# Splitting the activations of the first MoE into three tiles, one raw q buffer less, and a newly drawn order table

## The chip, the core and the metric

The kernel runs on one core of one Trainium2 chip. The metric is device time in microseconds (us) of one launch. The five engines that matter are TensorE (PE, with its weight loads as PEld), VectorE (DVE), ScalarE (ACT), GpSimd (POOL) and SyncE (SP), which only issues DMAs here; ACT issues some DMAs too.

## What is computed

Attention over 2 batches x 8 heads x 768 tokens x 64 with a hash mask (two tokens see each other only if the signs of six projections agree), then two feed-forward layers over the 1536 x 512 result:

```python
q_bucket = np.sum((np.einsum('bhsd,dk->bhsk', q, proj) > 0) * powers, axis=-1)   # k_bucket alike
scores = np.where(mask, scale * np.matmul(q, k.transpose(0, 1, 3, 2)), -1000000000.0)
attn = softmax(scores); x = attn @ v                              # 1536 x 512 after the heads are joined
h = np.maximum(np.maximum(x @ w1, x @ w2), x @ w3); x1 = h @ w_out  # first MoE, 512 -> 768 -> 512
h = x1 @ w_in; g = np.where(h > 0.0, h, np.exp(np.minimum(h, 0.0)) - 1.0); out = g @ w_out2   # 512 -> 2048 -> 512
```

All matmuls are made of pairs of f16 tiles (a rounded value and its remainder), so nearly each f32 result is followed by a cast to f16 and a subtraction that gives the remainder.

## The kernel before, in words

The work is cut into 6 chunks of 256 tokens. A chunk has 4 pairs of heads with 4 attention tiles each, so there are 96 attention tiles. One tile runs through: four score matmuls on PE into `s` (L596), the row maximum on DVE (L599) with two small scalings (L600, L602), the exponential on ACT into `P` (L604), the cast `hl` on ACT or DVE (L610, L612), the remainder `hl` on POOL or DVE (L615), a transposing DMA from SP into `PT` (L617), and 18 matmuls with v into `o` (L626 to L628). After two pairs the normalized result (`xn`, L648 and L649) is transposed into `xT`.

Ahead of that, `plan_qk` loads q (four heads, both pairs of two) and k (two heads), scales them, casts them into `natq` and `natk` with their remainders (L382, L384), transposes them on PE and makes the bits of the hash. `plan_v` does v, `plan_w13` and `plan_wo` split the weights of the first MoE, which DMAs load as `raww`.

`plan_moe1` takes one chunk: 18 up-projections of two blocks (in all 108 pieces of 12 matmuls, `mo<-xT,w`), three of which are joined by maxima on DVE into `hx` (L684; the first of three is a plain copy on ACT or DVE, L686 and L688), a cast (L693) and a remainder (L695) into `hT`, and 4 down-projections of 18 matmuls (`mo<-hT,wot`). `hT` is one tile for the whole chunk in a ring of one buffer: the next chunk's first cast has to wait for the last down-projection of the chunk before. The second MoE (`plan_moe2`, L759 on) follows when attention is closed.

The order of all this is written out. Every step is an operation with the engines that may run it; the string `ORDER` unpacks to a list of (operation, engine) pairs, and `emit` issues the program in that order, so each engine works in the order of the table and waits where a tile isn't there yet. SP and ACT issue DMAs in the same way: a DMA that waits holds up what the table puts behind it on its queue. Tiles come from rings with a number of buffers (`ring`, `Graph.buf`); in the kernel before, a ring's buffers go round in turn.

Of the kernel before, what the change touches and what calls it, by code (L numbers as in the profile page):

```python
# [12 lines left out]
F16 = mybir.dt.float16  # L13
# [4 lines left out]
ALU = mybir.AluOpType  # L18
# [12 lines left out]
class Graph:  # L31
# [5 lines left out]
    def buf(self, pool, shape, dt, tag, bufs, ordered=False):  # L37

        self.bufs_of[tag] = bufs
        b = Buf(tag, lambda: pool().tile(shape, dt, tag=tag, name=tag, bufs=bufs))  # L40
        return b

    def fixed(self, tile_, tag):

        self.bufs_of[tag] = 1
        return Buf(tag, lambda: tile_)
# [30 lines left out]
    def emit(self):  # L77

        raw = zlib.decompress(base64.b85decode(ORDER))
        n = len(raw) // 2  # L80
        assert n == len(self.ops)
        done = [False] * n
        for lo, hi in zip(raw[:n], raw[n:]):
            w = hi << 8 | lo
            o, e = self.ops[w >> 3], ENGINES[w & 7]
            assert e in o["eng"] and not done[o["i"]] and all(done[d] for d in o["deps"])
            done[o["i"]] = True
            for b in o["allocs"]:
                b.ap = b.make()
            o["fn"](e)  # L90
# [4 lines left out]
    "c-mD~O;{TD))(-DK~x6682n=Ji$P<=PX?m`Y9go+2r3w(fF^~s3-R`S9`R-&_AbQseI7Agi0vYnEW~CZHVd&?NScM%F2r^r_AbQRMKE26=|XH4?-}h~yl4LZbAIP{e&-Cs3?F48iBzG|KACkb8a;oU"  # L95
    "nZ1c5gwEpnUT*LLI~M=vGqWK)CqRV1M%}JoC8R=iWZv0}?(^+O%eTB%x7KF#to=DP<9|1MgvT!ezeim(J6g3^+pzK?SSUY^$<!B*;|ZE!CgfBzQB0^cv#q$;OPg|jr{_zSy)vcT=Vz;oqF?zN+iwVM"
    "^{ZjYae!3RrT>I;8e)QNDPLiZ&x@rAH<wf>)XQ}5?}RG;r1vdyH0f|2MpfOq?5{qxyt{no)9Q5bUmN0y!uyF`*<|<-JBYaGr%QA#jpdm!(rU@W+3C$U$di!??sJ#o<;mt}J1U*?^pDW6!4<~OL+)jB"
    "z`8PSmyLK&cGeuO5c<Zu5st{0yaH<=m<Xy0PWbcgai7*$w(0qo^}9W1jOE3@{_NHE>#5nWE9AB)5B86u2D8n!zARc;{aF-=N-WY3v313{=i|vgUb*K~W}ati(bfHA(=qAAFKvV;NwTG#db0V$+ik>q"
    "%J3b<WkEFN_+oSBP}#%A-bQ0qYkW4eYPUO_FE0ZEJ)xJ7x*zFF7Yi<T6saX?a|+eA=ZuN|tb7+&-xF?L2ErVJZXGj96cORlUR52sYfjj9Ld@VdcB3$7e+s3sX7+j5i0VbyLQF@7%?<O9BPYhXaocBN"
    "*__>JM|TUP3YXjT#acMxcL&aU4^PWhf*+y^RdhDSU)2sL3uvxOvD>ps?ly!tqRFr;5}h#*yD<E_S8gt*n?5BhwqFkC{*5epPLq&N<ICQUTk)tj7N0-&o!2S<S`#jQ?iYXmx-Q^3Nm@h^35s3H62aIr"  # L100
    "dPlO?w;~`|Yh<rqLefIhn+IFzR=Z=(zvTRDClpY==I?|Sj$@Z-TpeMek2Rv49d|hKPG^*?u9H8WslSqW?j?Og|5-Ts`qF4tFn@EXUtqR5hqG#nWu9_nqe0imK5xa(OA>@a;iZ+ZRLgR%y*VNZBljoj"
    "csQ{#dxD=le`#{L-yi>}^m}p?Q!!Pyc6c=qJWJHdNCyqUHN=#_Jp9kP-7p8kKmA-;rHh!l2}jhZy0D&FefIh9-F5R}t!4jwd3xh7&!66<h%p*_HoMxnE;~0l$T=PjQTkBV(yDE`!}a=`TG@_m&7a&G"
# [42 lines left out]
def vcopy(n): return n / 1.92 + 68  # L145
# [4 lines left out]
def act(n, ap=0, acc=0): return n / 1.2 + 93 + 93 * ap + 93 * acc  # L150
# [10 lines left out]
def lsh_attention_moe_kernel(ctx: ExitStack, tc: tile.TileContext, q, k, v, proj,  # L161
# [758 lines left out]
```

## Time and profile before

| | |
|---|---|
| median of 3 runs | 672.31 us (671.91 to 677.66) |
| the profiled execution | 675.43 us, its span 673.6 us |
| PE busy | 620.3 us, 92% of the span |
| DVE, ACT, POOL busy | 557.9, 439.1, 231.8 us |
| mean granted clock of TensorE | 0.976 |

The span runs from the first to the last instruction; the rest of an execution's time lies around it. Shares of busy time are means over stages that differ, so the stages are read one by one. A busy PE is not PE at its peak, since matmuls overlap and their ends are modelled.

### The profile page before, as it was taken

The page shows a single profiled execution, that of the slowest core. Times are in us where ns is not written, and L with a number is a line of the kernel's source. Part 1 is how long each engine was busy: PE and PEld are TensorE (multiplying, and loading weights), DVE is VectorE, ACT ScalarE, POOL GpSimd, SP SyncE. Part 2 cuts the span into 40 slices and gives each one's busy share as a digit, 9 for nine tenths or more (in the row PEclk, how much of TensorE's full clock was granted, in tenths as well). Part 3 has the DMA queues.
Part 4 walks back from the last instruction along what each step waited for, and adds up shares of the span by engine and source line. Part 5 has one row for each costly group of instructions (what it writes and reads, how often), then busy time and mean ns, then how long its engine had stood idle before and what let it go on. Part 6 is the DMA issues. An engine that isn't in the chain of part 4 may idle for free.

```text
span 673.6 us, 16529 instructions
## 1 busy us (share of the span) xinstructions
PE 620.3 (92%) x6414; PEld 479.0 (71%) x6414; DVE 557.9 (83%) x1541; ACT 439.1 (65%) x806; POOL 231.8 (34%) x198
## 2 busy tenths in 40 slices
PE   5777566989999999999999899999999999999997
PEld 4555454867888888788789788766676666676674
DVE  6898998979998887898884888888899897777584
ACT  4978786788887667767552667676677564343341
POOL 1263544566445656757651112021011111110110
PEclk9998777999999999999999999999999999999999
DMA  8899999977998777978985553432221000000102
GB/s 277 238 220 257 208 244 227 194 167 153 184 181 154 141 138 157 182 135 165 147 165 164 176 154 103 126 94 64 64 63 64 1 1 1 1 1 11 54 33 93
DMA packets 201119, 87.66 MB, mean 130 GB/s; under 512 B 167760, under 2 KB 195408, under 8 KB 201040
## 3 DMA queue, kind: packets, MB, share of 16 engines
q1 hardware_dynamic: 187860, 70.97, 49.5%
q10 hardware_dynamic: 13180, 15.63, 7.9%
q8 instruction: 50, 0.82, 0.6%
q14 instruction: 29, 0.24, 0.1%
HBM read 38.80 MB, written 3.15 MB: 62 GB/s over the span
## 4 chain that ended last, share of the span: by engine, by line
PE 73%; DVE 10%; DMA 8%; ACT 4%; issue 3%; POOL 1%; ACTq 0%; DVEq 0%; SPq 0%; POOLq 0%
PE mo L663 40%; PE out L799 18%; PE s L596 6%; DMA PT<-hl 6%; PE o L626 2%; PE o L627 2%; PE o L628 2%; DVE m L599 2%; DMA qb<-btq 2%; ACT P L604 1%; POOL hl L615 1%; PE mo L394 1%; DVE dc2w L520 1%; DMA rawk<-in_k_dram 1%; ACT junk L317 1%
## 5 line engine op out<-in xcount | busy, mean ns | idle before, releaser
L615 POOL TENSOR_TENSOR hl<-P,hl 128x768 f16<-128x768 f32 x84 | 140.9, 1682 | 125.2 <-ACT hl L610 65.3
L663 PE MATMUL mo<-xT,w 128*128 128x256 f16 x1296 | 152.3, 272 | 0.0
L663 PE MATMUL mo<-x1T,win 128*128 128x256 f16 x1152 | 136.1, 273 | 0.0
L663 PEld LDWEIGHTS <-w 128*128 128x128 f16 x1296 | 123.7, 98 | 16.5
L799 PE MATMUL out<-wo2t,gt 128*128 128x512 f16 x576 | 134.6, 379 | 0.0
L663 PEld LDWEIGHTS <-win 128*128 128x128 f16 x1152 | 112.0, 98 | 24.3
L604 ACT ACTIVATE P<-s,bias,scale 128x768 f32<-128x768 f32 x96 | 94.1, 987 | 31.9 <-DVE bias L602 24.8
L792 POOL TENSOR_TENSOR gt<-g,gt 128x256 f16<-128x256 f32 x50 | 34.9, 700 | 221.4 <-ACT gt L790 101.7
L599 DVE TENSOR_REDUCE m<-s 128x1 f32<-128x768 f32 x96 | 91.0, 951 | 16.4 <-PE s L596 14.8
L783 ACT ACTIVATE r<-mo,nih 128x256 f32<-128x256 f32 x96 | 45.1, 470 | 79.6 <-PE mo L663 73.1
L799 PEld LDWEIGHTS <-gt 128*128 128x128 f16 x576 | 55.2, 98 | 53.6
L596 PE MATMUL s<-ka,qa 128*128 128x384 f16 x192 | 52.6, 360 | 19.4 <-ACT P L604 19.2
L610 ACT CAST hl<-P 128x768 f16<-128x768 f32 x64 | 52.4, 829 | 27.5 <-DMA PT<-hl 21.7
L626 PE MATMUL o<-vt,PT 128*128 128x65 f16 x576 | 65.6, 200 | 2.9 <-DMA PT<-hl 2.3
L627 PE MATMUL o<-vt,PT 128*128 128x64 f16 x576 | 65.4, 200 | 0.0
L628 PE MATMUL o<-vt,PT 128*128 128x65 f16 x576 | 65.2, 199 | 0.0
L626 PEld LDWEIGHTS <-PT 128*128 128x128 f16 x576 | 56.2, 101 | 7.5 <-DMA PT<-hl 4.5
L786 DVE TENSOR_SCALAR uu<-e,sg 128x256 f32<-128x256 f32 x96 | 35.5, 369 | 28.9 <-ACT e L785 27.9
L627 PEld LDWEIGHTS <-PT 128*128 128x128 f16 x576 | 56.3, 102 | 2.4 <-issue 0.5
L628 PEld LDWEIGHTS <-PT 128*128 128x128 f16 x576 | 56.2, 103 | 0.0
L596 PE MATMUL s<-kb,qb 76*128 76x384 f16 x192 | 53.2, 362 | 1.3 <-DMA qb<-btq 1.3
L663 PE MATMUL mo<-hT,wot 128*128 128x256 f16 x432 | 50.2, 272 | 0.0
(195 smaller groups left out, 1080.0 us busy)
## 6 DMA issues: line engine op xcount, KB each, us to landing
raw<-in_moe_w_out_dram SPq DMA_DIRECT2D x11, 512.0 KB
raw<-in_moe_w_in_dram SPq DMA_DIRECT2D x10, 512.0 KB
raww<-in_moe_w_dram SPq DMA_DIRECT2D x9, 512.0 KB
raww<-in_moe_w_dram ACTq DMA_DIRECT2D x9, 512.0 KB
raw<-in_moe_w_in_dram ACTq DMA_DIRECT2D x6, 512.0 KB
out_dram<-ot SPq DMA_DIRECT2D x12, 256.0 KB
rawk<-in_k_dram SPq DMA_DIRECT2D x7, 384.0 KB
rawv<-in_v_dram SPq DMA_DIRECT2D x7, 384.0 KB
```

Of the source, the lines that this page charges most:

```text
L596: PE.matmul(ps.ap[:, h, :NK], lh[0:n, h0 + i, j], rh[0:n, i, h * CH:(h + 1) * CH], start=first, stop=not first)
L599: op({"V": vred(S)}, lambda e: V.tensor_reduce(out=m.ap, in_=ps.ap[:, :, :NK], op=ALU.max, axis=AX.XY), rd=[ps], wr=[m], prio=t + 80.5)
L604: op({"A": act(S, ap=2) - 42}, lambda e: A.activation(out=P.ap.rearrange("p (c n) -> p c n", c=2), in_=ps.ap[:, :, :NK], func=AF.Exp, scal ...
L610: A.copy(hl.ap[:, 0], P.ap)
L615: op({"G": gtt(S), "V": (vtt(S), -109.46)}, lambda e: eng[e].tensor_tensor(out=hl.ap[:, 1], in0=P.ap, in1=hl.ap[:, 0], op=ALU.subtract), r ...
L626: PE.matmul(oo, pt.ap[:, kt], vt.ap[:, i, kt, :D + 1], start=(kt == 0), stop=False)
L627: PE.matmul(oo[:, :D], pt.ap[:, kt], vt.ap[:, i, kt, D + 2:], start=False, stop=False)
L628: PE.matmul(oo, pt.ap[:, NS + kt], vt.ap[:, i, kt, :D + 1], start=False, stop=(kt == NS - 1))
L663: PE.matmul(o, lh(kk, x), rh(kk, y), start=(kk == 0 and pi == 0), stop=(kk == n - 1 and pi == 2))
L783: op({"A": act(NQ, ap=1) - 42}, lambda e, m=m, o=o, r=r: A.activation(out=r.ap, in_=o.ap[:, :NQ], func=AF.Relu, scale=nih.ap[:, m:m + 1]), ...
L786: op({"V": vts(NQ)}, lambda e, m=m, ex=ex, uu=uu: V.tensor_scalar(out=uu.ap, in0=ex.ap, scalar1=-1.0, scalar2=sg.ap[:, m:m + 1], op0=ALU.a ...
L799: PE.matmul(outs[j].ap, gt.ap[:, x, j * 128:(j + 1) * 128], wo2t[f].ap[:, y], start=(len(seen) == 1 and pi == 0), stop=(len(seen) == n and ...
```

## The change

Four things change. The activations `hT` of a chunk become three tiles of two blocks each: the first from a ring `hTa`, the other two from a ring `hTb`, each with two buffers. The ring of raw q has one buffer where it had two; the raw buffers of k and v stay at two. A ring is now a set of separate tiles, and the buffer that an operation gets is the free slot, or the one whose last use stands earliest in the table. The table itself is new: all operations are the same, but their order, and for many the engine, differs.

```diff
-        b = Buf(tag, lambda: pool().tile(shape, dt, tag=tag, name=tag, bufs=bufs))
+        b = Buf(tag, lambda slot: pool().tile(shape, dt, tag=f"{tag}{slot}", name=f"{tag}{slot}", bufs=1))
...
+                slots, last = held[b.ring], max(place[i] for i in b.users)
+                if len(slots) < self.bufs_of[b.ring]:
+                    slot = len(slots)
+                    slots.append(last)
+                else:
+                    slot = min(range(len(slots)), key=slots.__getitem__)
+                    assert slots[slot] < t
+                    slots[slot] = last
+                b.ap = b.make(slot)
...
-        raw = ring(at, [128, heads, n, D], "raw" + kind, 2, ordered=True)
+        raw = ring(at, [128, heads, n, D], "raw" + kind, 1 if kind == "q" else 2, ordered=True)
...
-        hT = ring(hp, [128, FM, 2, NQ], "hT", 1, F16)
+        hT = [ring(hp, [128, 2, 2, NQ], "hTb" if f else "hTa", 2, F16) for f in range(0, FM, 2)]
...
-               rd=[t], wr=[hT], two=True, prio=pr + -417.89)
+               rd=[t], wr=[hT[f // 2]], two=True, prio=pr + -417.89)
...
-                    rd=[hT] + [f"wo{f}" for f in range(FM)], wr=[o, t], prio=pr + h * 1.5 * dp + 7.99)
+                    rd=hT + [f"wo{f}" for f in range(FM)], wr=[o, t], prio=pr + h * 1.5 * dp + 7.99)
```

Counted over the whole program, the new table moves 11 of the 96 remainders `hl` and 9 of the 18 remainders `hT` from POOL to DVE, 7 casts `hl` from DVE to ACT, and smaller numbers of other steps either way. PE has the same 12,830 instruction rows, and the last 3,053 of them stand in the same order as before. Line numbers of the changed kernel are 10 higher than before from `emit` on (L615 is L625 there).

The first place is the start of SP's queue, which issues the first loads. Before:

```order
L372 DMA rawq<-in_q_dram 128x4x128
L372 DMA rawk<-in_k_dram 128x2x384 x2
L471 DMA rawv<-in_v_dram 128x2x384
L372 DMA rawq<-in_q_dram 128x4x128
L505 DMA raww<-in_moe_w_dram 128x4x256
L471 DMA rawv<-in_v_dram 128x2x384
L372 DMA rawk<-in_k_dram 128x2x384
L505 DMA raww<-in_moe_w_dram 128x4x256
```

The same place in the changed kernel:

```order
L382 DMA rawq_153<-in_q_dram 128x4x128
L382 DMA rawk_170<-in_k_dram 128x2x384
L481 DMA rawv_186<-in_v_dram 128x2x384
L382 DMA rawk_198<-in_k_dram 128x2x384
L382 DMA rawq_205<-in_q_dram 128x4x128
L481 DMA rawv_272<-in_v_dram 128x2x384
L515 DMA raww_275<-in_moe_w_dram 128x4x256
L515 DMA raww_293<-in_moe_w_dram 128x4x256
L382 DMA rawk_304<-in_k_dram 128x2x384
```

Behind the second `rawq` stand now two loads for v and the weights; with one buffer that load waits until the first q has been split into `natq`, and SP waits with it.

The second place is the first MoE's remainder, in the middle of the attention stretch. Before, on POOL, among the remainders `hl` of the attention tiles (numbers tell tiles apart):

```order
L615 TENSOR_TENSOR hl_4041<-P_3954,hl_4041 128x768
L615 TENSOR_TENSOR hl_4086<-P_3900,hl_4086 128x768
L695 TENSOR_TENSOR hT_3740<-hx_3836,hT_3740 128x2x256
L615 TENSOR_TENSOR hl_4132<-P_3985,hl_4132 128x768
L695 TENSOR_TENSOR hT_3740<-hx_4114,hT_3740 128x2x256
L384 TENSOR_TENSOR natk_4031<-rawk_3459,natk_4031 128x12x64
L615 TENSOR_TENSOR hl_4255<-P_4173,hl_4255 128x768
```

In the changed kernel, on DVE, among the row maxima and scalings of attention tiles (L609, L610, L612) and the sums for v:

```order
L705 TENSOR_TENSOR hTb0_4004<-hx2_3820,hTb0_4004 128x2x256
L312 TENSOR_SCALAR vs1_99<-mo0_4117 128x1
L612 TENSOR_SCALAR bias0_4121<-m2_4089,scale0_4091 128x1
L499 TENSOR_REDUCE vm1_101<-vs1_99 128x1
L314 TENSOR_SCALAR vs1_99<-vs1_99 128x1
L694 SCALAR_TENSOR_TENSOR hx0_4095<-mo1_4094,hx1_4023 128x512
L703 CAST hTb1_4175<-hx0_4095 128x2x256
L705 TENSOR_TENSOR hTb1_4175<-hx0_4095,hTb1_4175 128x2x256
```

The remainders `hTb` stand on DVE right behind their cast or their maximum (L694), where POOL made them before.

The third place is PE near the end of attention, where the fifth chunk's sum of squares (`hacc`, which sets the scale of its down-projection) is made with a matmul by `ones`. Before:

```order
L264 LDWEIGHTS ones
L264 MATMUL mo<-hacc,ones 128x1
L265 LDWEIGHTS ones
L265 MATMUL mo<-tinyc,ones 128x1
L663 LDWEIGHTS wot
L663 MATMUL mo<-hT,wot 128x256
```

The same place in the changed kernel:

```order
L274 LDWEIGHTS ones
L274 MATMUL mo_7352<-hacc_7128,ones 128x1
L275 LDWEIGHTS ones
L275 MATMUL mo_7352<-tinyc,ones 128x1
L673 LDWEIGHTS w_104
L673 MATMUL mo_7325<-xT_6903,w_104 128x256
```

Before, the down-projection (`hT,wot`) followed at once; now one piece of the next chunk's up-projection (`xT`, 12 matmuls) stands between, and one more stands ahead of the sum.

## Rows read from the trace of the kernel before

**Rows 1.** The page: the span in 40 slices, busy tenths; PEclk is the granted clock.

```profile
PE   5777566989999999999999899999999999999997
...
PEclk9998777999999999999999999999999999999999
```

**Rows 2.** Windows: us of each engine's busy time per stretch, instructions in brackets, clock, DMA share.

```profile
core 0: us, PE busy (x) PEld busy (x) DVE busy (x) ACT busy (x) POOL busy (x), PEclk, DMA share, GB/s
0.00:60.00 60.00, 40.24 (x484) 31.18 (x485) 49.56 (x146) 44.26 (x73) 20.87 (x27) 1.00 0.94 242
60.00:110.00 50.00, 33.80 (x389) 24.42 (x389) 46.79 (x122) 42.17 (x68) 25.76 (x17) 0.69 1.14 240
110.00:157.00 47.00, 38.55 (x517) 32.11 (x516) 39.49 (x105) 36.08 (x56) 25.23 (x17) 1.00 0.89 186
157.00:350.00 193.00, 190.78 (x2585) 163.10 (x2583) 166.56 (x416) 141.71 (x215) 115.12 (x79) 1.00 0.85 157
350.00:425.00 75.00, 72.13 (x720) 62.45 (x719) 58.05 (x165) 44.16 (x99) 11.58 (x11) 1.00 0.51 150
425.00:674.00 249.00, 244.77 (x1729) 165.71 (x1726) 197.48 (x592) 130.74 (x300) 33.22 (x48) 1.00 0.13 43
```

**Rows 3.** The chain that ended last, 95 to 165: start, us, what.

```profile
108.88 6.62 DMA PT<-hl
...
151.34 4.91 DMA PT<-hl
...
157.02 1.31 PE mo L663 x12
...
158.88 0.65 PE s L596 x4
```

**Rows 4.** Groups by line and form: count, busy us, mean ns of one, idle before.

```profile
L615 DVE TENSOR_TENSOR hl<-P,hl 128x768 f16<-128x768 f32 x12 | 13.2, 1099 | 0.4 <-ACT hl L610 0.3
...
L612 DVE CAST hl<-P 128x768 f16<-128x768 f32 x32 | 19.4, 608 | 1.6 <-ACT P L604 0.9 <-DMA PT<-hl 0.4 <-DMA qb<-btq 0.2
...
L695 DVE TENSOR_TENSOR hT<-hx,hT 128x512 f16<-128x512 f32 x3 | 2.6, 858 | 0.0
...
L688 DVE TENSOR_SCALAR hx<-mo 128x512 f32<-128x512 f32 x2 | 1.4, 692 | 1.9 <-PE mo L663 1.9
...
L615 POOL TENSOR_TENSOR hl<-P,hl 128x768 f16<-128x768 f32 x84 | 140.9, 1682 | 125.2 <-ACT hl L610 65.3 <-DVE hl L612 32.9 <-issue 11.3
```

**Rows 5.** Two lines alone: shortest, median and longest of their instructions, in ns.

```profile
L615 DVE TENSOR_TENSOR hl<-P,hl x12: 943/950/1932, 81.1 to 354.9; 128x768 f16<-128x768 f32 x12
...
L612 DVE CAST hl<-P x32: 545/554/1517, 34.6 to 354.3; 128x768 f16<-128x768 f32 x32
```

**Rows 6.** Timeline of PE, 368 to 386: start, us, instruction, idle before and its releaser.

```profile
375.27 0.16 PE L264 MATMUL mo<-w2acc,ones 128*128 128x1 bf16 x1 [0.78 <-ACT junk L317]
...
376.02 0.16 PE L264 MATMUL mo<-hacc,ones 128*128 128x1 bf16 x1 [0.52 <-ACT junk L317]
...
378.87 0.16 PE L264 MATMUL mo<-w2acc,ones 128*128 128x1 bf16 x1 [0.67 <-ACT junk L317]
...
383.73 0.18 PE L264 MATMUL mo<-w2acc,ones 128*128 128x1 bf16 x1 [0.72 <-DVE hx L717]
```

**Rows 7.** Timeline, 0 to 16: the first loads from SP, and the first q split.

```profile
3.12 0.47 SPq L372 DMA_DIRECT2D rawq<-in_q_dram  x1
...
7.31 0.69 DVE L384 TENSOR_TENSOR natq<-rawq,natq 128x512 f16<-128x512 f32 x1
...
11.05 0.37 SPq L372 DMA_DIRECT2D rawk<-in_k_dram  x1
```

**Rows 8.** Waits of the queue of SP, 0 to 157: us in total, times, longest.

```profile
SPq L617 <- POOL natq L384: 6.2, 3, 3.3
...
SPq L372 <- POOL natq L384: 1.8, 1, 1.8
```

**Rows 9.** Timeline of PE, 655 to 674: its last piece.

```profile
660.58 9.23 PE L799 MATMUL out<-wo2t,gt 128*128 128x512 f16 x42
```

More of the change, by code (lines that the diff above doesn't have):

```diff
@@ L45, in fixed @@
         self.bufs_of[tag] = 1
-        return Buf(tag, lambda: tile_)
+        return Buf(tag, lambda slot: tile_)
     def op(self, eng, fn, rd=(), wr=(), prio=0.0, two=False):
@@ L81, in emit @@
         assert n == len(self.ops)
-        done = [False] * n
-        for lo, hi in zip(raw[:n], raw[n:]):
-            w = hi << 8 | lo
+        place, held = {}, defaultdict(list)
+        todo = [(hi << 8 | lo) for lo, hi in zip(raw[:n], raw[n:])]
+        for t, w in enumerate(todo):
+            place[w >> 3] = t
+        for t, w in enumerate(todo):
             o, e = self.ops[w >> 3], ENGINES[w & 7]
-            assert e in o["eng"] and not done[o["i"]] and all(done[d] for d in o["deps"])
-            done[o["i"]] = True
+            assert e in o["eng"] and all(place[d] < t for d in o["deps"])
             for b in o["allocs"]:
-                b.ap = b.make()
+                slots, last = held[b.ring], max(place[i] for i in b.users)
[7 more added lines that the diff above has]
+                b.ap = b.make(slot)
             o["fn"](e)
@@ L99 @@
[L99 to L102, printed above, removed]
@@ new lines @@
+    "-aq8apG3}g{lQQsCyc}xEDVjrIdj6q?!lX537%A{zhpY}n0eAUukrrsTD83u24~jOzh4@{kw05}B>%iuwM?5qePVxb?-=_`QTeS|b0TuTOtr)sS2^h^IZa~Bkc#9c)n(B0dnmkPQ!CV@lN3ejSQrqX"
+    "zor*mU&u3L8QZ7aT#f2~o>m7Xq1Sq98J)MYKj+3pM{&L9i1TZuQiGY($)w)4_m=V6a^+1Q{<e}7zD>&v_#ZJg`|Q!=j(_%>Ov1w_?Z)CtD&vS0PNiSjKIHb3Po-j$@F%>^Fy{3+lneIh&A^^bZE$2<"
+    "nU737w{LDfX4{$Db<706#UinIG#;TY%_qFCgJfS~brn55dv9TTyoz5#U%pxkVuI7xYJKv+Y+v7d7nA($JX_rICX%TOpI`RmBmbc<DA=BI9jAYgvwqo_349ig{50*p%Eg4r&v$6*mwQ`!$$~s**^kUE"
+    "24~#9km^V^m)z<{Q1;R*iPp$VrLST;E0G^bMFzcN-hOToO7LII!ONv9m1$q>awnbPgoi}gSyD6YD|FoaR;jk@G1O_8T^ak>w!lx{VrPCbJDsj4(v7Hwbnumj#rIoW6qTCFKwrMuWw&^JiT#;aJis%U"
@@ new lines @@
+    "g^9RKxo!^}o#N`XBzJDXX-|D5to!!0)Eb`mR{A1(i{I@*Nzr|&VB0HCz4yKO``>YI!cJa8M874^lyvrm<3ra4wmKU;5K5=f^~_Nsx$(*JUwPrkVNUWz$`9AG$WEsJ;=v_fctqRsUX*<i6n?iCAcwZr"
+    "CAh@F-X--6NW!YC81e%@b~Q^qIps%oV+N+~ttN%$q*Ih1f3YAt=x&DWTJ}@V9}4i`dXC%dS(+NlNN}Z1<8;}k!){NR=GG6C6?FTHgRfq)_TI!-4BnMQG?qh+KS~^a%Cc6@9m`lVO7*1P!~2hA9u2PV"
+    "3qt`+*dO)=!rpIAPU8`dJ&`<nr<10lug-n`j2j_gAO5)(7xG-6EMOaME8Xj`Uo3uixyi<a4$BWx!-3D^kuUz`R|Rjm5=rrF9tlC^D~VLk0KPiE@xprHWO@JFEM1$$RiO^?%C1_zPVwu)2mQU_tF<>A"
+    "rwem${FhK7-;BhgN4X2kW3%mhZ>|1Bm9w^=jQkW$r8B3eDgn(&roNL<@H3^WF&^H3zAZ%0qh(*mGzRfiW$3+X+O56veCn0uC||5BBP@EH9XI!5$3}hNn_1CI^UiN#9DAiyU!9s)4e#vz9<R?73J09K"
@@ L142 @@
+    "(S+GYW41?QkH)U;adu7GpFw&$_SiuXj~{2*$AE2cj6*#>{`fi(_V~JZJo(s`h2u6b`%{~p$hL9FcKf*fp9Lk@<fMJlZoftVCZ9}BK6&!Q{?8&p)+Zr8efH#u<H=KCK?3S0lTRm~K79%q5ctzc2f;w+"
+    "*>(NI0qv*Ho?gdigk8rhA{vk#5F8(T@IiKgIUU#LbU2;Qi0T;>A3THN83>+bmCg_T8Tbb|ub~s1*yH~Ilz|{_"
 )
@@ L692, in plan_moe1 @@
                 prev = t
-            op({"V": vcopy(N2), "A": (act(N2), -91.99)}, lambda e, f=f, t=t: (V.tensor_copy if e == "V" else A.copy)(hT.ap[:, f:f + 2, 0], two_(t)),
-               rd=[t], wr=[hT], two=True, prio=pr + -417.89)
+            op({"V": vcopy(N2), "A": (act(N2), -91.99)}, lambda e, f=f, t=t: (V.tensor_copy if e == "V" else A.copy)(hT[f // 2].ap[:, :, 0], two_(t)),
+               rd=[t], wr=[hT[f // 2]], two=True, prio=pr + -417.89)
             op({"G": gtt(N2), "V": (vtt(N2), 391.34)}, lambda e, f=f, t=t: eng[e].tensor_tensor(
-                out=hT.ap[:, f:f + 2, 1], in0=two_(t), in1=hT.ap[:, f:f + 2, 0], op=ALU.subtract), rd=[t, hT], wr=[hT], two=True, prio=pr + 159.76)
+                out=hT[f // 2].ap[:, :, 1], in0=two_(t), in1=hT[f // 2].ap[:, :, 0], op=ALU.subtract), rd=[t, hT[f // 2]], wr=[hT[f // 2]], two=True, prio=pr + 159.76)
             square(t, lambda t=t: t.ap, N2, bufcol(hacc, f // 2), pr)
```

82 lines of the change are left out of this document (38 added, 44 removed).

## The prediction

> **What bounds the kernel now.** I read the page's slices first, then windows by stage, then the chain of waits. The slices of PE show three stages: a front in which PE is busy for five to eight tenths, a long stretch at nine, and an end at nine and a short tail [rows 1]. The windows give the amounts [rows 2]. Up to 157 us PE is idle for 60 - 40.24 = 19.8, 50 - 33.80 = 16.2 and 47 - 38.55 = 8.5 us, 44.4 in all, and from 60 to 110 its clock was granted at 0.69 on average, so for a good part at the lower of its two levels, 1.2 GHz. From 157 to 350 PE is idle for 2.2 us only, from 350 to 425 for 2.9, from 425 to the end for next to nothing but the 4 us after its last matmuls, which end near 669.8 [rows 9]. Matmul work is the same before and after, so the time can change only through the start of the saturated stretch, through the 5.1 us of gaps in it, or through new gaps. In the front DVE is the busiest engine: 49.56 of 60, 46.79 of 50, 39.49 of 47 us [rows 2]. It is idle for 10.4, 3.2 and 7.5 us there. From 60 to 110 it is the bound; from 110 to 157 the chain of waits passes through the transposing DMAs of the attention tiles, 4.91 and 6.62 us a piece in the rows shown, with the last one just before the first up-projection at 157.02 [rows 3].
>
> **What the change moves, and the sum.** I counted the new table's instructions on each engine up to the same attention tile and gave each the mean of its line and form [rows 4].
>
> *Front, DVE.* Up to the 25th row maximum DVE has 3.6 us more work than before, with two remainders `hl` moved over from POOL (2 x 1.099 = 2.2 us) as the largest item; the rest is scalings and splits of weights and raw tiles, and casts that went the other way. ACT has 4.4 us less, POOL the same. The place of the first up-projection in PE's order is one tile later, behind 26 score and 20 value pieces instead of 25 and 19. Where DVE is the bound (60 to 110, 3.2 us of idle time) the 3.6 us must be paid; in the 7.5 us of idle time behind 110 they can be hidden, by work that waits for transposes there. Bounds: +5.3 (all of it and more; the sum up to the 26th maximum is 5.3) and -7.5 (a table that fits the transposes better closes all that idle time). I take half of 3.6, +1.8.
>
> *One tile earlier.* The tile that now lies ahead of the first up-projection is work that the saturated stretch no longer has: its scores took 0.65 us, and its 18 matmuls with v fill the 0.55 us between the end of the up-projection piece at 158.33 and the scores at 158.88 [rows 3]. -1.2.
>
> *Middle, DVE.* From the 25th to the 96th row maximum DVE gets 9.9 us more: nine remainders `hl` (9.9), eight `hT` (6.9) and five first copies `hx` (3.5) come over, six casts `hl` (3.6) and a number of raw scalings, splits and casts (near 6.8 net) leave. POOL loses 24.7 us over the whole program, but it isn't waited for much: it is busy for 115.12 of 193 us [rows 2]. DVE is idle for 26.4 of those 193 us; the cover shrinks to 16.5. If PE's waits grow as the cover shrinks, 2.2 us become 2.2 x 26.4 / 16.5 = 3.5. I take +1.3, with bounds 0 (all hidden; each remainder is ready 1.682 - 1.099 = 0.6 us sooner [rows 4]) and +9.9 (none hidden, where the moved steps stand in front of a row maximum that PE's next scores wait for through ACT).
>
> *Gaps near 375.* PE waits four times for sums of squares or for the tile ahead of them, 0.78 + 0.52 + 0.67 + 0.72 = 2.7 us [rows 6]. In the new order two pieces of the sixth chunk's up-projection stand around the fifth chunk's sum, before its down-projection; a piece is 1.31 us [rows 3]. This covers the first two waits, -1.3; the other two are for the weights of the second MoE, which I leave. Bounds 0 and -2.7.
>
> *The q buffer.* The second q load, issued at 3.12 us, now waits for the end of the first q's split at 7.31 + 0.69 = 8.0, and two loads wait behind it on SP. The old queue stood still too, till 11.05 [rows 7]; the first weights also come by ACT's queue. On DVE the work up to the fourth row maximum is 3.4 us less than before. I take 0, between +3 (the load late by 4.9, less what the old stop hid) and -3.4.
>
> *Split tiles and rings by rule.* These issue no instruction. In the table the down-projections of the first four chunks still stand ahead of all up-projections of the next; the second buffers of `hTa` and `hTb` serve the late stretch above. The last 3,053 rows of PE, about from 440 us on, are unchanged: 0.
>
> Sum: +1.8 - 1.2 + 1.3 - 1.3 = +0.6. The profiled execution, 675.43 us, becomes 676.0; it lies 3.1 above the median of the runs, 672.31, so the forecast in terms of the median is **672.9 us**. A change under 1% (665.6 to 679.0) is about what a measurement of this kernel can't tell from none.
>
> **A rule against the trace.** The remainder on DVE took 950 ns in the median and up to 1932, the cast 554 and up to 1517 [rows 5]: some of them stand still for about a microsecond. The Trainium skill, page "SBUF — State Buffer", section "Who interferes with whom", says that a DVE instruction with two SBUF inputs and a GpSimd instruction that reads SBUF block each other for the whole of an instruction. The trace agrees as far as those longest cases go. By that rule every remainder moved to DVE meets those still on POOL, and at the worst length the eleven moved `hl` would cost 11 x (1.932 - 1.099) = 9.2 us more on DVE. By the mean of the row, which has such cases in it, nothing is added to the sum; and POOL's smaller share gives some of it back.
>
> **The rivals.**
>
> *DVE becomes the bound of the attention stretch (slower).* For it: 46.79 of 50 us before 110, and 86% rising to 91% from 157 to 350. Against it: 26.4 us of cover. It decides when the moved remainders stand ahead of row maxima at the wrong moment, so that half of their 9.9 us shows: 5.3 - 1.2 + 5.0 = +9.1 and no gain at 375, 681.4; with all of it 686. Chance 0.24, of which a fifth stays under 1%. The port rule above acts through this place too.
>
> *The front closes (faster).* For it: the chain runs through transposes and the casts and remainders around them, a remainder on DVE is ready sooner, ACT has 4.4 us less there, and the first row maxima come after less work. Against it: DVE has more. The first up-projection comes 7.5 us sooner: -7.5 - 1.2 - 2.7 + 1.3 = -10.1, 662.2. Chance 0.30, of which a sixth stays within 1%.
>
> *SP stands before a q load (slower).* With one buffer a load of q waits for the split of the group before. SP already stood for POOL's `natq` three times for 6.2 us, up to 3.3 at once, ahead of transposes [rows 8]. Two of the new q loads on SP lie among the front's transposes; 2 x 3.3 = +6.6 on top of the sum, 679.5. Against it: in most places the table has the split well ahead of the load. Chance 0.06.
>
> *The change does nothing that counts*: the buffers stay unused and the order evens out, 672.3; together with the forecast, 0.40.
>
> Within 1%: 0.40 + 0.05 + 0.05 + 0.02 = 0.52. Faster: 0.25. Slower: 0.23. The likeliest case's own range is 666 to 679; the range that should hold 8 of 10 reaches to the middle of the two main rivals' further parts, 661.5 to 684.
>
> **What would show it.** Windows of the changed kernel: the first `xT,w` piece between 155 and 160; PE idle between 2 and 5 us from there to 350; DVE busy for 9 to 11 us more in all, POOL for some 25 less; waits of PE near 375 down to about 1.4. The forecast is wrong if the first piece comes before 152 or after 163, if PE's waits in the middle pass 8 us, or if SP's waits for `natq` exceed 12 us in the front.

## The result, and the profile after

The changed kernel takes 678.75 us in the median of 20 runs (673.29 to 684.31), the kernel before 674.6 us in 20 runs beside it (671.91 to 678.08). The ratio is 1.0054, 95% interval 1.0034 to 1.0075: slower by about 3.6 us, and within the 1% that the forecast called no change. The ratio leaves out two of the changed kernel's runs, which lie more than 1.5% above its fastest, so it is a little nearer to 1 than the quotient of the medians. The profiled execution took 676.24 us, its span 674.4. Executions of one kernel lie up to 11 us apart, so the two profiles (span 673.6 before) show where time goes, and the ratios how much.

The page after, the slices that answer to [rows 1]:

```profile
PE   4766666999999999999999999999999999999997
...
PEclk9966687999999999999999999999999999999999
```

The first, third and fourth slices of PE are a tenth emptier, and the clock of the third and fourth was granted at 6 where 9 and 8 stood. Then the windows that answer to [rows 2], same columns:

```profile
core 0: us, PE busy (x) PEld busy (x) DVE busy (x) ACT busy (x) POOL busy (x), PEclk, DMA share, GB/s
0.00:60.00 60.00, 36.88 (x441) 28.12 (x441) 45.91 (x144) 38.94 (x62) 17.55 (x24) 0.88 0.91 237
60.00:110.00 50.00, 33.16 (x372) 23.46 (x373) 43.87 (x108) 41.01 (x64) 22.32 (x14) 0.67 1.00 213
110.00:157.00 47.00, 43.25 (x555) 35.22 (x553) 44.93 (x124) 40.75 (x60) 26.05 (x18) 0.96 0.98 210
157.00:350.00 193.00, 188.93 (x2523) 160.62 (x2521) 166.71 (x416) 146.24 (x226) 94.72 (x66) 1.00 0.85 158
350.00:425.00 75.00, 74.77 (x795) 65.23 (x794) 57.12 (x160) 46.53 (x99) 13.33 (x13) 1.00 0.59 155
425.00:674.00 249.00, 245.54 (x1737) 166.53 (x1734) 198.24 (x600) 135.40 (x309) 33.71 (x49) 1.00 0.13 43
```

From 0 to 60 us PE was busy for 3.4 us less and DVE for 3.7 us less; from 110 to 157 both were busy for about 5 us more. From 157 to 350 PE is idle for 193 - 188.93 = 4.1 us instead of 2.2, from 350 to 425 for 0.2 instead of 2.9.

The timeline of PE gives the first up-projection (start, us, instruction). Before:

```profile
112.51 1.47 PE L663 MATMUL mo<-xT,w 128*128 128x256 f16 x12
```

After:

```profile
121.81 2.78 PE L673 MATMUL mo<-xT,w 128*128 128x256 f16 x24
```

This is the place that the prediction read wrongly: its 157.02 us [rows 3] is the first piece that the chain of waits holds, not the first one on PE. The chain lists only its own pieces.

The loss arises earlier. DVE starts row maximum 7 at 47.3 us before and 47.9 after, 8 at 51.2 and 56.5, 10 at 57.0 and 66.0, 25 at 113.0 and 120.5. PE from 44 to 57 us after, with the idle time before an instruction and what ended it:

```profile
49.51 0.51 PE L404 MATMUL mo<-ident,natk 128*128 128x128 f16 x6 [0.37 <-POOL natk L394]
52.75 0.23 PE L636 MATMUL o<-vt,PT 128*128 128x65 f16 x1 [2.73 <-DMA PT<-hl]
...
53.73 0.20 PE L274 MATMUL mo<-gm,ones 128*128 128x1 bf16 x1
...
54.82 0.83 PE L404 MATMUL mo<-ident,natk 128*128 128x128 f16 x6
55.44 0.65 PE L606 MATMUL s<-ka,qa 128*128 128x384 f16 x2
```

And DVE over the same time:

```profile
49.55 0.68 DVE L530 SCALAR_TENSOR_TENSOR dc2w<-mo,dc2w 128x512 int32<-128x512 int32 x1
54.00 0.16 DVE L312 TENSOR_SCALAR swm<-mo 128x1 int32<-128x1 int32 x1 [3.77 <-PE mo L275]
...
56.45 0.96 DVE L609 TENSOR_REDUCE m<-s 128x1 f32<-128x768 f32 x1 [0.24 <-PE s L606]
...
63.44 0.95 DVE L609 TENSOR_REDUCE m<-s 128x1 f32<-128x768 f32 x1
```

A value piece (`o<-vt,PT`, the 18 matmuls of a tile with v) heads PE's queue and waits 2.73 us for its transposing DMA. Behind it stand a sum (L274) that DVE waits for, 3.77 us, six k transposes (L404) and the scores of tile 8 (L606), none of which need that `PT`. Counted from 44 to 110 us (wait: us in total, times, longest), the waits of value pieces for `PT` are new. After:

```profile
PE o L636 <- DMA PT<-hl: 10.7, 4, 3.4
...
DVE swm L312 <- PE mo L275: 6.6, 2, 3.8
PE s L606 <- ACT P L614: 5.4, 7, 2.1
```

Before, this wait isn't among PE's; the longest in total there is the scores' for the exponential, which after is down to 5.4 us:

```profile
PE s L596 <- ACT P L604: 10.1, 8, 3.9
```

Groups by line and form after, which answer to [rows 4]:

```profile
L625 DVE TENSOR_TENSOR hl<-P,hl 128x768 f16<-128x768 f32 x23 | 22.2, 968 | 0.7 <-ACT hl L620 0.3 <-issue 0.2
...
L622 DVE CAST hl<-P 128x768 f16<-128x768 f32 x25 | 13.9, 554 | 5.6 <-DMA PT<-hl 4.0 <-ACT P L614 1.3
...
L705 DVE TENSOR_TENSOR hTb<-hx,hTb 128x512 f16<-128x512 f32 x9 | 6.2, 694 | 0.4 <-ACT hTb L703 0.2
...
L698 DVE TENSOR_SCALAR hx<-mo 128x512 f32<-128x512 f32 x5 | 3.4, 675 | 0.0
...
L625 POOL TENSOR_TENSOR hl<-P,hl 128x768 f16<-128x768 f32 x73 | 123.4, 1697 | 143.0 <-ACT hl L620 82.7 <-DVE hl L622 33.7 <-issue 8.7
```

The counts moved as the prediction says, and POOL's busy time fell by 24.1 us to 207.7. But DVE's did not rise: 556.8 us after 557.9. The mean of a remainder fell from 1099 to 968 ns, that of a cast from 608 to 554. With the mean of each form as before, the counts of after would give about 10 us more. The typical instruction is no shorter, though; the two lines alone after (shortest, median, longest), against [rows 5]:

```profile
L625 DVE TENSOR_TENSOR hl<-P,hl x23: 946/951/1311, 70.0 to 357.0; 128x768 f16<-128x768 f32 x23
...
L622 DVE CAST hl<-P x25: 546/552/561, 31.4 to 355.5; 128x768 f16<-128x768 f32 x25
```

The medians are the same (950 and 554 before). What fell is the number of long ones: two remainders of 12 before (1741 and 1932 ns), one of 23 after (1311); three casts of 32 before (786 to 1517), none of 25 after. The longest remainder of before began while POOL worked:

```profile
349.46 1.16 POOL L721 TENSOR_TENSOR x1T<-hx,x1T 128x512 f16<-128x512 f32 x1 [1.33 <-ACT x1T L719]
349.50 1.93 DVE L615 TENSOR_TENSOR hl<-P,hl 128x768 f16<-128x768 f32 x1
```

PE near 375 us after, which answers to [rows 6]: of the four waits one is left.

```profile
378.37 0.17 PE L274 MATMUL mo<-w2acc,ones 128*128 128x1 bf16 x1
...
379.73 0.17 PE L274 MATMUL mo<-w2acc,ones 128*128 128x1 bf16 x1
...
380.13 0.16 PE L274 MATMUL mo<-hacc,ones 128*128 128x1 bf16 x1 [0.16 <-ACT junk L327]
...
383.45 0.17 PE L274 MATMUL mo<-w2acc,ones 128*128 128x1 bf16 x1
```

SP's waits from 0 to 157 us, which answer to [rows 8]:

```profile
SPq L382 <- DVE natq L394: 3.8, 1, 3.8
...
SPq L627 <- POOL natq L394: 2.6, 1, 2.6
```

The load of q now waits for its split for 3.8 us in one piece instead of 1.8, the transposes behind `natq` for 2.6 instead of 6.2; together 6.4 instead of 8.0.

### The profile page after: what moved, and what is told of

The parts are those of the page before. It is cut to its first block, busy times and chain, and to the rows that moved or that the text cites. A ratio compares the mean times of both kernels' runs of the same rounds, so it can differ in the third digit from the quotient of the medians.

```text
span 674.4 us, 16552 instructions
## 1 busy us (share of the span) xinstructions
PE 622.5 (92%) x6414; PEld 479.2 (71%) x6414; DVE 556.8 (83%) x1546; ACT 448.9 (67%) x816; POOL 207.7 (31%) x183
## 4 chain that ended last, share of the span: by engine, by line
PE 62%; DMA 15%; DVE 9%; ACT 7%; issue 3%; POOL 2%; ACTq 0%; SPq 0%; DVEq 0%; POOLq 0%
PE mo L673 34%; PE out L809 18%; DMA PT<-hl 12%; PE s L606 4%; ACT P L614 2%; POOL hl L625 2%; DVE m L609 2%; ACT hl L620 2%; DMA rawk<-in_k_dram 2%; PE o L636 1%; PE o L637 1%; PE o L638 1%; ACT junk L327 1%; PE mo L404 1%; DMA raw<-in_moe_w_in_dram 1%
## 5 line engine op out<-in xcount | busy, mean ns | idle before, releaser
L625 POOL TENSOR_TENSOR hl<-P,hl 128x768 f16<-128x768 f32 x73 | 123.4, 1697 | 143.0 <-ACT hl L620 82.7
L609 DVE TENSOR_REDUCE m<-s 128x1 f32<-128x768 f32 x96 | 91.0, 951 | 10.0 <-PE s L606 8.0
L636 PE MATMUL o<-vt,PT 128*128 128x65 f16 x576 | 66.9, 200 | 15.5 <-DMA PT<-hl 13.2
L636 PEld LDWEIGHTS <-PT 128*128 128x128 f16 x576 | 56.5, 102 | 20.3 <-DMA PT<-hl 15.1
L637 PE MATMUL o<-vt,PT 128*128 128x64 f16 x576 | 66.9, 201 | 0.0
L638 PE MATMUL o<-vt,PT 128*128 128x65 f16 x576 | 66.7, 200 | 0.0
L620 ACT CAST hl<-P 128x768 f16<-128x768 f32 x71 | 58.2, 827 | 7.9 <-DMA PT<-hl 6.9
L606 PE MATMUL s<-ka,qa 128*128 128x384 f16 x192 | 52.4, 358 | 11.6 <-ACT P L614 11.1
L606 PE MATMUL s<-kb,qb 76*128 76x384 f16 x192 | 52.7, 359 | 1.1 <-DMA kb<-btk 1.1
L798 DVE SCALAR_TENSOR_TENSOR g<-mo,aj,uu 128x256 f32<-128x256 f32 x96 | 46.1, 481 | 4.9 <-POOL gt L802 0.9
```

Source lines behind the costliest of these rows:

```text
L606: PE.matmul(ps.ap[:, h, :NK], lh[0:n, h0 + i, j], rh[0:n, i, h * CH:(h + 1) * CH], start=first, stop=not first)
L609: op({"V": vred(S)}, lambda e: V.tensor_reduce(out=m.ap, in_=ps.ap[:, :, :NK], op=ALU.max, axis=AX.XY), rd=[ps], wr=[m], prio=t + 80.5)
L620: A.copy(hl.ap[:, 0], P.ap)
L625: op({"G": gtt(S), "V": (vtt(S), -109.46)}, lambda e: eng[e].tensor_tensor(out=hl.ap[:, 1], in0=P.ap, in1=hl.ap[:, 0], op=ALU.subtract), r ...
L636: PE.matmul(oo, pt.ap[:, kt], vt.ap[:, i, kt, :D + 1], start=(kt == 0), stop=False)
L637: PE.matmul(oo[:, :D], pt.ap[:, kt], vt.ap[:, i, kt, D + 2:], start=False, stop=False)
```

## The experiments

All are built on the changed kernel's code; only the table and, where the old table needs it, the buffers differ. With the old table or a part of it, raw q has two buffers again and `hTa` one:

```diff
-        raw = ring(at, [128, heads, n, D], "raw" + kind, 1 if kind == "q" else 2, ordered=True)
+        raw = ring(at, [128, heads, n, D], "raw" + kind, 2, ordered=True)
-        hT = [ring(hp, [128, 2, 2, NQ], "hTb" if f else "hTa", 2, F16) for f in range(0, FM, 2)]
+        hT = [ring(hp, [128, 2, 2, NQ], "hTb" if f else "hTa", 2 if f else 1, F16) for f in range(0, FM, 2)]
```

Every ratio is to the kernel before on the same chip, with its 95% interval; two of these runs compared with each other mostly ran on different chips. A ratio isn't the quotient of two medians: they differ by up to 0.34%. Times of tiles are from one profiled execution each.

### Structure, buffers, and the two ends of the table

Four runs, with these tables:

```diff
-ORDER = new
+ORDER = old                                                  # old_table
+ORDER = new, and the edit above                              # new_q2
+ORDER = old[:622] + [x for x in new if x not in old[:622]]   # front_old: old to its 25th tile
+ORDER = new[:676] + [x for x in old if x not in new[:676]]   # front_new: new to its 28th tile
```

Old table on the new structure.

> The order table of the kernel before, on the new structure: hT split in three tiles (one buffer of hTa, two of hTb, the room of the old tile), rings as separate tiles given out by rule, two raw q buffers. Theory (the table makes the difference, first of all its front): as before, 0 to 1 us off 674.6. Rival (the split and the rule for buffers change waits by themselves): 2 us or more off.

Two raw q buffers under the new table.

> The new table with two raw q buffers; the room comes from the second hTa buffer, which is taken away. Rival theory (the single raw q buffer holds up SP and with it the front): the 25th row maximum comes 4 us or more sooner than in the changed kernel (120.5 us), and the time falls to 675 or less. Theory (order of the front, not the buffer): as the changed kernel, 677 to 680, the 25th row maximum within 2 us.

Old front, new rest.

> The old table up to its 25th attention tile, then all that is left in the order and on the engines of the new table. Theory (the new front costs, the new end gains 3 to 5 us near 375): 670 to 673. Rival (the 10 us more of DVE work between tile 25 and 96 cost): 676 to 679.

New front, old rest.

> The new table up to its 28th attention tile, then what is left in the order and on the engines of the old table. Theory (the new front costs, and here nothing gives it back near 375): 678 to 682, slower than the changed kernel or like it. Rival (DVE's work in the middle costs): 674 to 676, as before.

| run | median, us | ratio |
|---|---|---|
| old table throughout | 675.31 | 1.0014 (0.9989 to 1.0039) |
| new table, two raw q buffers | 676.20 | 1.0042 (1.0015 to 1.0069) |
| old front, new rest | 670.57 | 0.9963 (0.9942 to 0.9983) |
| new front, old rest | 679.89 | 1.0127 (1.0080 to 1.0174) |

The split tiles and the rings by rule cost nothing that can be measured. The second q buffer, for which one buffer of `hTa` was given up, brings nothing that can be told from noise: 676.20 lies just under the 677 to 680 of the theory, and the 25th row maximum starts at 122.0 us, not sooner than in the changed kernel.

The new front with the old rest costs 1.27%, 8.6 us (5.4 to 11.7). This figure has only six runs behind it, five at 679.0 to 680.7 and one at 688.42; the medians differ by 6.3 us. With the new rest, the new front (1.0054) against the old one (0.9963, and 0.9937 when repeated below) costs 0.91 and 1.17%, 6.1 and 7.9 us. So the new front costs some 6 to 9 us, and the rest of the new table gives part of it back.

The windows of before and after don't show this size, since the new order behind the front puts more matmuls ahead of 157 us. Counted from the rows of the traces, the four profiles with the old front and the new order behind it have started matmuls of 177 to 178 thousand columns by 157 us, `end_new` (below; nearly all old) 174, the changed kernel 168 and `new_q2`, with the same order, 161.5. A piece of 12 matmuls of 256 columns takes 1.31 us [rows 3], so the new front is 4 to 7 us behind in these profiles, by estimate.

### Is it the front's order, its engines, or one wait?

`front_engines` takes the run with the new front and puts every step on the engine of the old table:

```diff
-ORDER = front_new
+ORDER = [(step, engine of step in old) for step in front_new]
```

> The new table's order up to its 28th tile and the old order behind it (the run that took 1.0127 of the kernel before), but every step on the engine that the old table gave it: only the order of the front is new. Theory (the order costs the time: what stands in front of what on PE, SP and DVE): the ratio stays at 1.009 or more. Rival (the engines cost it: 3.6 us more work on DVE up to the 25th row maximum): half or more of the 1.27% goes, ratio 1.006 or less.

It took 694.51 us, 1.0294 (1.0264 to 1.0324). So taking the moved work off DVE again gives nothing back: with the old engines the new order is far slower than with its own. This speaks against the moved work as the front's loss, but it doesn't price the engines by themselves, since the old order on the new engines was not run.

`pe_move` is the changed kernel with two value pieces moved behind the scores on PE:

```diff
  k transposes x6 (L404)
- value piece of a tile (L636 to L638), which waits for its PT
  sums (L274, L275)
- value piece of a tile
  k transposes x6, scores of tile 8 (L606), q transposes x8
+ value piece
+ value piece
```

> The changed kernel with one edit in its table: the two value pieces that stood on PE at 52.8 and 53.9 us, ahead of the sums, the k transposes and the scores of the eighth tile, now stand behind those scores and the q transposes that follow; two small DVE steps that use their result stand some steps later too. Nothing else moves. Theory (the wait of 2.73 us for a transposing DMA in front of the sums, through which DVE then stands for 3.77 us, is part of what the new front costs): DVE's wait for the sum falls under 1 us, row maximum 10 comes at 62 to 64 us instead of 66.0, and the time falls by about 3 us, ratio to the kernel before 0.998 to 1.003. Rival (the front's extra work on DVE sets its end, and a wait taken away in one place comes back in the next): row maximum 10 within 1 us of 66.0 or the 25th within 1 us of 120.5, ratio 1.004 to 1.007 as without the edit.

It took 675.05 us, 0.9996 (0.9972 to 1.0020), so 0.58% less than the changed kernel's 1.0054, which was measured on another chip. DVE from 47 to 59 us in this run's timeline:

```profile
48.62 0.15 DVE L312 TENSOR_SCALAR swm<-mo 128x1 int32<-128x1 int32 x1
...
50.73 0.94 DVE L609 TENSOR_REDUCE m<-s 128x1 f32<-128x768 f32 x1
...
57.60 0.84 DVE L530 SCALAR_TENSOR_TENSOR dc2w<-mo,dc2w 128x512 int32<-128x512 int32 x1
58.37 0.94 DVE L609 TENSOR_REDUCE m<-s 128x1 f32<-128x768 f32 x1
```

The sum is there at 48.62 without a wait, row maximum 8 starts at 50.73 instead of 56.45, and the tenth at 61.1 instead of 66.0. Three profiles with this front unmoved (`after`, `new_q2`, `front_new`) have the eighth maximum at 56.5, 55.7 and 54.1 us, three with the two pieces moved (`pe_move` and the next two runs) at 50.7, 50.2 and 50.5. At the 25th the lead of `pe_move` is down to 1.3 us (119.2 against 120.5), but the three unmoved profiles lie from 117.7 to 122.0 there, so a single profile decides nothing at that place; the profiled execution of the changed kernel lies 2.5 us under its median, this one 0.6 us over. Only the runs, 20 and 12 of them, say that the lead lasts (0.58%, give or take 0.3). The theory is borne out by the time and by the early maxima.

### What is left of the front's loss

`pv_late` moves seven more value pieces of the front in the same way:

```diff
- value pieces 10 to 16 in front of the scores of tiles 17, 18 and 20 and of a sum
+ two behind scores 17, one behind 18, two behind 20, two behind the sum
```

> The run that took 0.9996 of the kernel before (two value pieces moved behind the scores on PE), and in the same way seven more value pieces of the front, among them three that waited for a transposing DMA in front of scores or a sum (2.1 us at 85.7, 1.7 us at 95.4 and 3.5 us at 105.9 us of that run): each now stands behind the next scores, or behind the next sum. Theory (the value pieces that stand too early in the queue of PE are the front's loss): the three waits fall together by 4 us or more, the 25th row maximum comes before 117 us instead of at 119.2, and the ratio falls to 0.992 to 0.997. Rival (once the largest stall is gone the transposes themselves, 6 to 8.6 us each, set the pace, and the waits move to the next scores, whose P or row maximum isn't there): ratio 0.998 to 1.002.

It took 675.64 us, 1.0015 (0.9988 to 1.0041): no gain over `pe_move`. PE's waits from 44 to 110 us, first in `pe_move`:

```profile
PE o L636 <- DMA PT<-hl: 9.6, 3, 4.0
PE s L606 <- ACT P L614: 5.2, 6, 2.1
```

And in `pv_late`:

```profile
PE s L606 <- ACT P L614: 9.3, 7, 2.6
...
PE o L636 <- DMA PT<-hl: 5.4, 3, 3.9
...
PE mo L425 <- DVE dc2w L530: 3.7, 1, 3.7
```

The waits for `PT` fall by 4.2 us, and those of scores and projections for ACT and DVE rise by about 8. The time and these waits are as the rival said; the fall of the waits for `PT` and the early 25th maximum are as the theory said, but they didn't bring the time. The profiled execution alone would mislead: it took 670.80 us with the 25th maximum at 115.1, and the median of the 12 runs is 4.8 us longer.

`rowmax_early` goes at DVE's seven microseconds between maxima 8 and 9:

```diff
  row maximum 8, scalings
+ row maximum 9, scalings          (and its scores ahead of the two value pieces on PE)
  weight splits, raw q, hash bits
- row maximum 9, scalings
```

> The run that took 0.9996 of the kernel before (two value pieces moved behind the scores of the eighth tile), and on top of it the scores, row maximum, scalings and exponential of the ninth tile, and the scores and row maximum of the tenth, moved ahead of six to ten steps on weights, raw q and hash bits, which stood on DVE between the row maxima at 50.7 and 58.4 us in that run; DVE does the same steps, later. Theory (the rest of the front's loss, 0.9996 against 0.9963 with the old front, is this order on DVE): row maximum 9 comes 4 us or more sooner after row maximum 8 (7.7 us before), the 25th before 117 us, and the ratio is 0.993 to 0.997. Rival (the same work has to be done by DVE before the next q and k are there, so the gain is given back at the next tiles): the ninth maximum is early, the 25th within 1.5 us of 119.2, ratio 0.998 to 1.003.

The scores and the maximum of tile 10 moved up too. It took 681.67 us, 1.0097 (1.0062 to 1.0133). Neither theory: the edit made a wait of its own. The timeline of PE from 51 to 60 us:

```profile
56.65 0.80 PE L606 MATMUL s<-kb,qb 76*128 76x384 f16 x2 [5.64 <-DMA kb<-btk]
```

And of DVE:

```profile
57.49 0.96 DVE L609 TENSOR_REDUCE m<-s 128x1 f32<-128x768 f32 x1 [5.24 <-PE s L606]
```

The scores of tile 9 need a piece of `kb` that was still on its way; they hold PE for 5.64 us and DVE for 5.24. So the run says nothing of the loss that is left. The whole edit, with this wait in it, cost 1.0097 - 0.9996, about 6.8 us, give or take 3; as other steps moved too, that is no clean price of the wait.

### The middle and the end

`end_new` keeps the old table until nearly all of attention is placed; only its last part is new:

```diff
-ORDER = new
+ORDER = old[:1899] + [x for x in new if x not in old[:1899]]
```

> The old table until all but the last pieces of attention are placed, then the new table's order: of the new table only what stands from about 350 us on is left. Theory (the new end fills PE's gaps near 375 us and the table's middle gives nothing): the idle time of PE from 350 to 425 falls from 2.9 us to under 1, and the ratio is 0.994 to 0.998. Rival (the gain behind the front comes from the new middle): ratio 1.000 to 1.004, as with the old table throughout (1.0014).

It took 671.69 us, 0.9968 (0.9940 to 0.9996). Its window that answers to the fifth of [rows 2]:

```profile
350.00:425.00 75.00, 74.53 (x746) 65.16 (x745) 58.02 (x167) 45.58 (x100) 8.10 (x8) 1.00 0.51 149
```

PE is idle for 0.5 us there instead of 2.9. Old front and new end are worth as much as old front, new middle and new end, as far as the intervals tell.

`mid_pool` and `mid_hT_pool` take the run with the old front and put moved remainders of the middle back on POOL:

```diff
 hl remainders (L625), 15 of them:  -DVE +POOL      # mid_pool
 hT remainders (L705), 9 of them:   -DVE +POOL      # mid_pool and mid_hT_pool
```

Both kinds.

> The old table up to its 25th tile and the new order behind it (the run that took 0.9963 of the kernel before), with 15 remainders hl and 9 remainders hT that the new table put on DVE set back to POOL, where the old table had them; places in the order stay. Theory (in the middle the choice between DVE and POOL for a remainder moves no bound, because PE is saturated there): ratio 0.995 to 0.998, DVE busy about 20 us less and POOL 40 us more. Rival 1 (the moved remainders cost time in the middle): 0.993 or less. Rival 2 (they are what makes the new middle fast, since POOL at 1.7 us a remainder stands in front of transposes): 1.000 or more.

The `hT` alone.

> The old table up to its 25th tile and the new order behind it (0.9963), with the 9 remainders hT alone set back to POOL; the 15 remainders hl stay on DVE (both together took 1.0098). Theory (the moved remainders hl are what counts, since a transpose and then PE's value piece wait for each, and a remainder takes 1.68 us on POOL and 0.97 on DVE): ratio 0.995 to 1.000. Rival (the hT are what counts, since they stand on POOL in front of remainders hl): ratio 1.004 or more.

Both took 682.70 us, 1.0098 (1.0063 to 1.0134); the `hT` alone 673.28 us, 0.9968 (0.9939 to 0.9997). The theory for `mid_pool`, that the choice moves no bound, failed, and its second rival came true; that for the `hT` alone held. So the engine of the `hT` shows no effect (0.9968 against 0.9963), and by difference it is the `hl` on DVE that count: putting them back costs about 1.3%. The `hl` alone were not run. `mid_pool` also leaves POOL more remainders `hl` than either kernel, 90 against 84 before and 73 after. The middle in the run with the old front, then in `mid_pool`:

```profile
157.00:350.00 193.00, 190.74 (x2558) 162.60 (x2556) 167.30 (x416) 146.35 (x227) 93.70 (x66) 1.00 0.87 159
350.00:425.00 75.00, 74.74 (x740) 64.54 (x738) 58.19 (x167) 46.92 (x104) 11.16 (x11) 1.00 0.55 154
```

```profile
157.00:350.00 193.00, 185.52 (x2435) 156.42 (x2433) 152.29 (x377) 139.29 (x215) 119.47 (x83) 0.99 0.81 150
350.00:425.00 75.00, 72.92 (x773) 63.37 (x771) 56.76 (x154) 46.38 (x98) 16.34 (x14) 1.00 0.61 163
```

DVE has 15 us less to do from 157 to 350, and PE waits for 7.5 us instead of 2.3 (4.9 in the other profile of the run with the old front). The groups of `mid_pool`, and the remainders on DVE alone:

```profile
L622 DVE CAST hl<-P 128x768 f16<-128x768 f32 x25 | 15.6, 624 | 7.9 <-DMA PT<-hl 5.5 <-ACT P L614 1.5 <-DMA qb<-qa 0.7
...
L625 DVE TENSOR_TENSOR hl<-P,hl 128x768 f16<-128x768 f32 x6 | 6.8, 1128 | 1.0 <-ACT hl L620 1.0
...
L625 DVE TENSOR_TENSOR hl<-P,hl x6: 941/946/2033, 83.1 to 359.9; 128x768 f16<-128x768 f32 x6
```

With POOL busy for 246.5 us the means are 624 ns for the cast and 1128 for the remainder, again with the same medians (559 and 946): five casts of 25 take 690 to 1409 ns, one remainder of six 2033.

`front_old_again` repeats the best version (diff as for `front_old`).

> The old table up to its 25th tile and the new order behind it, once more (0.9963 of the kernel before the first time), beside the other run on the same chip. Theory (the new order behind the front is worth 0.3 to 0.4%, about what the gaps near 375 us give): 0.994 to 0.998. Rival (the first value was a lucky one): 0.999 or more.

It took 670.39 us, 0.9937 (0.9907 to 0.9968). The two intervals overlap from 0.9942 to 0.9968, and the rival, a lucky first value, is out. This version beats both kernels: the old order for the first 25 tiles, the new one behind.

## Why the forecast held, and where its steps didn't

**The forecast**, no change, with +0.6 us, came out at +0.54%, 3.6 us. Its terms were off by more than that, with both signs, so that the sum stayed so near is in part luck: the front cost 6 to 9 us where +0.6 stood, and what lies behind it gave back 2 to 4 where +1.3 and -1.3 stood.

**Front, DVE (+1.8) and one tile earlier (-1.2).** This pair failed. The new front costs +8.6 us by `front_new`, 6 to 9 by all comparisons, where the upper bound of the DVE term was +5.3. The prediction counted how much work stands on DVE ahead of a maximum and split it by idle time; moving that work back to the old engines makes it worse (`front_engines`). What it left out is what stands at the head of a queue while it waits; about half of the loss is shown to be that. In the new order a value piece stands ahead of sums and scores and its transpose isn't there. Moving two pieces takes back 0.58% of the kernel's time (`pe_move`), some 3.9 us, give or take 2, for a wait of 3.77 us on DVE. The prediction looked at PE's order only around the up-projection, at a place that was misread; its sign "between 155 and 160" rested on that place, and the first piece came at 112.51 before and 121.81 after. The "one tile earlier", which was priced at the same misread place, doesn't show in any run.

**Middle, DVE (+1.3).** The sign is open: old front with new middle and end (0.9963, 0.9937) lies 0.3 and 2.1 us under old front with new end alone (0.9968), less than the intervals. PE's idle time from 157 to 350, 4.1 us, was within the foretold 2 to 5. But the sign that DVE would be busier by 9 to 11 us did not come: POOL works 24.1 us less, and on DVE fewer instructions are held up. The prediction weighed the rule of the Trainium skill's page "SBUF — State Buffer", section "Who interferes with whom", by which a DVE instruction with two SBUF inputs and a GpSimd instruction that reads SBUF block each other. The trace agrees for the long remainders: the four over 1.1 us in the profiles of before, after and `mid_pool` each began while a POOL instruction ran, and were longer than the median by 0.79, 0.98, 0.36 and 1.09 us, where that instruction still had 0.92, 1.12, 0.49 and 1.22 us to go. A remainder that had begun 0.7 us ahead of a POOL instruction (at 293.17 us after) took 949 ns, no more than the median. The casts over 650 ns in these profiles, too, each began while a POOL instruction ran. With POOL busy for 207.7, 231.8 and 246.5 us, 1 remainder of 23, 2 of 12 and 1 of 6 were so long, and of the casts none of 25, 3 of 32 and 5 of 25. The prediction feared from it 9.2 us more, as if every remainder moved met one on POOL; but a remainder on DVE takes 0.97 us of DVE in the mean and removes 1.68 us of POOL, and so makes such meetings fewer. Within the new order the place matters: `mid_pool` is 1.3% slower than the run with the `hl` on DVE.

**Gaps near 375 (-1.3).** Right in mechanism, too small: the other two waits, which it left as they were, went too, since the new order puts other pieces ahead of those sums (84 matmuls of the up-projection ahead of the one at 378.37). PE's idle time from 350 to 425 fell by 2.6 us, and the new end alone is worth 0.3% (0.9968), about 2 us, interval 0.3 to 4.

**The q buffer (0), split tiles and rings (0).** Right: 1.0042 with the second buffer against 1.0054 without, overlapping intervals, and 1.0014 for the old table on the new structure.

**The rivals.** DVE did not become the bound of the attention stretch: it is idle for 193 - 166.71 = 26.3 us there, as before. The front did not close but opened. SP stood before a q load for 3.8 us at once, about what the rival had assumed, but the waits for `natq` fell in sum, and `new_q2` shows no price for them.

In sum: +8.6 for the front (+6.3 by the medians), of which 3.9, give or take 2, is one wait, and between -2.2 (`end_new`) and -4.2 us (`front_old_again`) behind it. Together that is +4.4 to +6.4 (+2.1 to +4.1), where 3.6 (2.3 to 5.1) was measured; the intervals of the parts cover the rest. **Open** is what the other half of the front's loss is. The waits for `PT` at 69, 86 and 106 us of `pe_move` are there, but with seven more pieces moved the waits went elsewhere, and the edit on DVE's order made a wait of its own.

## What to carry to other kernels

Read a new order at the head of each queue: for every instruction that waits for a DMA, list what stands behind it on its engine and doesn't need that DMA, and who waits for those. A sum of moved work by idle time misses this; here one such wait of 3.8 us on DVE was worth 3.9 us of the kernel, give or take 2. A table's order and its choice of engines belong together, while its stretches can be swapped: trying the parts of two tables apart found the better kernel.

## What was not expected of the hardware

Some 10 us of work moved to DVE didn't show in its busy time, since fewer of its instructions ran long; POOL was busy for 24.1 us less. That the long ones began behind a running POOL instruction is shown for the remainders and casts of the attention tiles alone. And the granted clock up to 60 us doesn't follow the front's order: it was 1.00 in the profiles before and of `end_new`, but 0.82 in that of `front_old_again`, which has the same first 25 tiles and the shortest times, and 0.88 after. So the lower clock there isn't what makes the new front slow.
